# Where the weight conversions stand in ScalarE's queue: paced by key/value evictions and by gate sigmoids

## The chip, the cores and the metric

The kernel runs on one core of one Trainium2 chip. The metric is the time of one execution in microseconds (us), as the device measures it. TensorE (PE) multiplies matrices, VectorE (DVE), ScalarE (ACT) and GpSimd (POOL) do elementwise work, and SyncE (SP) issues the transfers. Each engine takes its own instructions strictly in the order of its own list. The order of these lists is made when the program is built: a scheduler sorts the instructions by priorities and by the dependences that the code declares.

## The reference

Three layers follow one another, on 4 batches of 576 positions, with 512 features (8 heads of 64):

```
x  = attention(rotate(q), rotate(k), v)            # 8 heads, softmax over 576 positions
xk = mu_k*x + (1-mu_k)*x_prev ; xr = mu_r*x + (1-mu_r)*x_prev   # x_prev: x one position earlier
x  = sigmoid(xr @ w_r) * (relu(xk @ w_k)**2 @ w_v)               # 512 -> 1024 -> 512, and the gate
u  = x + (relu(x^T @ w_tok1) @ w_tok2)^T                         # token mixing, 576 -> 256 -> 576
out = u + relu(u @ w_ch1) @ w_ch2                                # channel mixing, 512 -> 1536 -> 512
```

The weights come as 64-bit floats. The kernel turns each into a pair of a high and a low part, and every product of that kind is made of three matmuls (high x high, high x low, low x high).

## The kernel before, in words

Each batch is cut into two halves of 288 positions, which gives 8 chunks. The span has four stretches. Up to about 417 us attention runs, with the key/value products of chunks 0 to 4 in between. Then come the key/value products of chunks 5, 6 and 7 ("K/V stage", `kvr_gen`), then the gate and token mixing of the batches ("gate stage", `gate_gen` and `tok_gen`), and from about 605 us channel mixing (`ch_gen`).

For a chunk of the K/V stage, four slices `xs` of the mixed input are made, each on a chain `a`, `f`, `xs` high, `xs` low over ACT, DVE and POOL. TensorE makes 8 accumulators `kp` of 12 matmuls each. ScalarE evicts each with a Relu into `t` and squares it into the high part of `k`; POOL squares it again into `q`, and the low part of `k` is `q` minus the high part (on POOL for chunk 5, on DVE for chunks 6 and 7). TensorE then makes 4 accumulators `vp` of 24 matmuls, which ScalarE evicts into `vt`. There are four PSUM buffers for these accumulators.

For the gate, each batch half needs four slices `xs` by such a chain, in which the buffers `a` and `f` exist once, so that a new `f` waits until POOL has read the one before. Then 4 accumulators `rp` of 12 matmuls follow, each evicted by a Sigmoid into `q`. Token mixing of a batch is a chain of transposes (`trp`, evicted into `ytk`), products `t1p` (into `h`) and products `t2p` (added to `y` on DVE), in two halves.

A weight piece is converted in `Conv.stage` in four steps. It is loaded into `words` (SP). ScalarE copies it into a buffer `cv` (L215 of before); three DVE instructions put the bits together (L222, L226, L228). ScalarE writes the high part into `parts`, and DVE subtracts to get the low part (L111). Pieces of the channel weights also have their largest value taken (L233, a few tiny ones), and are scaled by it (L82 on ScalarE, L246 on DVE). `Conv.step` issues the next step of two pieces. `cv` has three buffers.

The group "conv1" is issued during the K/V stage and "conv2" during the gate stage. `SPREAD` sets how much K/V work is emitted between two steps of conv1, and the loop on `PACE` and `STEP` how much gate and token work between two steps of conv2. This is the order in which the code emits them; the scheduler may place them elsewhere. `Conv` has a means against that: where `after` names an entry of `last`, the ScalarE copy of a piece is put behind the instruction that the entry holds when the step is emitted. No engine waits more by it, it is only an order in ScalarE's list.

Of the kernel before, what the change touches and what calls it, by code (L numbers as in the profile page):

```python
# [13 lines left out]
AF = mybir.ActivationFunctionType  # L14
# [14 lines left out]

PV_AT = {7: 0, 12: 1}  # L30

HELD, LATE = 5, 2

UNIT = [(0, 256), (256, 320)]

# [1 line left out]

CW, HALF, TWICE = DCH // 2, KC // 2, 3

PACE, STEP, REST, SPREAD = (24, 28), 1, 8, 60  # L40

RAW, LOW = 3, "P"

# [28 lines left out]
def body(tc, kin, qin, vw, tabs, ident, mu, w_k, w_v, w_r, w_t1, w_t2, w_c1, w_c2, out):  # L72
# [41 lines left out]
    with ctx:  # L114
# [634 lines left out]
        def kvr_gen(seq, ready):  # L749

            xs_of = {}
            ld_of = {}

            def load(n):
                if n < len(seq) and n not in ld_of and ready(seq[n]):
                    kind, b, c = seq[n]
                    ld_of[n] = xT[b]
                    xs_of[n] = []

            def lerp(n):  # L760
                if (n < len(seq) and n in ld_of and len(xs_of[n]) < KD
                        and seq[n][1] * NP + len(xs_of[n]) in a_done):
                    xs_of[n].append(lerp_slice(ld_of[n], seq[n][2] * HS, len(xs_of[n]), 0))

            pend = []

            def tick():
                for x in pend:
                    x[0] -= 1
                while pend and pend[0][0] <= 0:  # L770
                    pend.pop(0)[1]()

            def later(*fs):
                for n, f in fs:
                    pend.append([n, f])
                pend.sort(key=lambda x: x[0])

            for n, (kind, b, c) in enumerate(seq):
                while n not in ld_of:
                    load(n)  # L780
                    tick()
                    yield 0
                if len(xs_of[n]) < KD:
                    if not xs_of[n]:
                        yield 0
                    while len(xs_of[n]) < KD:
                        lerp(n)
                        tick()
                        yield 0
                while n == HELD and not wide:  # L790
                    tick()
                    yield 0
                xs = xs_of[n]
                k2 = [None] * KF
                for m in range(KF):
                    p = accps("kp")
                    for kk in range(KD):
                        with ahead(PRI["kvpe"]):
                            mm3(p[:, 0:HS], wk[m // 4][kk], m % 4, xs[kk], kk == 0, kk == KD - 1)
                        tick()  # L800
                        yield 3

                    def ev1(p=p, m=m):
                        k2[m] = P["t"].tile([128, HS], F32, tag="t", name="t")
                        act.activation(out=k2[m], in_=p[:, 0:HS], func=AF.Relu)  # L805

                    def ev2(m=m):
                        t, k2[m] = k2[m], P["k2"].tile([128, 2, HS], F32R, tag="k2", name="k2")
                        act.activation(out=k2[m][:, 0], in_=t, func=AF.Square)
                        q = P["q"].tile([128, HS], F32, tag="q", name="q")  # L810
                        tt("P", q, t, t, ALU.mult)
                        tt("D" if second else "P", k2[m][:, 1], q, k2[m][:, 0].bitcast(F32), ALU.subtract)
                    later((1, ev1), (2, ev2))
                load(n + 1)
                half.append(n)
                for m in range(KD):
                    p = accps("vp")
                    for kf in range(KF):
                        with ahead(PRI["kvpe"]):
                            mm3(p[:, 0:HS], wv[kf // 4][kf % 4], m, k2[kf], kf == 0, kf == KF - 1)  # L820
                        if kf == 1:
                            load(n + 1)
                        if kf == 4:
                            lerp(n + 1)
                        tick()
                        yield 3

                    def ev(p=p, m=m, b=b, c=c):
                        vt = P["vt"].tile([128, HS], F32, tag="vt", name="vt")
                        copy("A", vt, p[:, 0:HS])  # L830
                        sp.dma_start(vd[b][c][:, m], vt)
                    later((1, ev))
            while pend:
                tick()
# [141 lines left out]
        def cv_t():  # L976
            return cv_p.tile([128, S], I32, tag="cv", name="cv")

        c2_a = c2_part(0, HALF)
        cv = Conv(cv_t, [wr, t1, t2], "conv1", low="D", then="out")  # L980
        def gate_gen(b):

            y = y_p[b].tile([128, KD, S], F32, tag="y", name="y")
# [3 lines left out]
            for c in range(2):  # L987
                o = c * HS
                sp.dma_start(y[:, :, o:o + HS], vd[b][c])
                yield 1  # L990
                xs = []
                for kk in range(KD):
                    a = P["a"].tile([128, HS], F32, tag="a", name="a")
                    copy("A", a, x[:, kk, o:o + HS], om_s[:, 1, kk:kk + 1])
                    f = P["f"].tile([128, HS], F32, tag="f", name="f")
                    dve.scalar_tensor_tensor(out=f, in0=x[:, kk, o + 1:o + HS + 1], scalar=mu_s[:, 1, kk:kk + 1], in1=a,
                                             op0=ALU.mult, op1=ALU.add)
                    if c == 0:
                        t = P["xs"].tile([128, 2, HS], F32R, tag="xs", name="xs")
                    else:  # L1000
                        if kk % 2 == 0:
                            two = M["uhl"].tile([128, 2, 2, HS], F32R, tag="uhl", name="xs")
                        t = two[:, kk % 2]
                    copy("A", t[:, 0], f)
                    tt("P", t[:, 1], f, t[:, 0].bitcast(F32), ALU.subtract)
                    xs.append(t)
                    yield 2
                cc = slice(c * HS, (c + 1) * HS)

                def fin(m, p):  # L1010
                    q = P["q"].tile([128, HS], F32, tag="q", name="q")
                    act.activation(out=q, in_=p[:, 0:HS], func=AF.Sigmoid)
                    tt("P", y[:, m, cc], q, y[:, m, cc], ALU.mult)

                for m in range(KD):
                    p = tps("rp")
                    for kk in range(KD):
                        mm3(p[:, 0:HS], wr[kk], m, xs[kk], kk == 0, kk == KD - 1)
                    fin(m, p)
                    yield 12  # L1020
# [33 lines left out]
        c2_b = c2_part(HALF, KC)  # L1054
        for nm, n in (("ytk", 1), ("h1", 2), ("uhl", 2), ("hs", 3), ("ht", 2), ("st", 2), ("top", 1)):
            M[nm] = top("m_" + nm, n)
        cv, cv3 = Conv(cv_t, [c1_w[0], c2_a], "conv2", low="D"), Conv(cv_t, [c1_w[1], c2_b], "conv3", low="D", after="hs")
        def all_max(m):

            p = tps("mp")  # L1060
# [144 lines left out]
        while B - 1 not in g_done or B - 2 not in u_done or not cv.done():  # L1205
# [1 line left out]
            if B - 2 not in u_done:  # L1207
                tok.advance(PACE[1])
            n += 1
            if n % STEP == 0 and not cv.done():  # L1210
                cv.step()
        n = 0
        ch = Stream(ch_gen())
# [78 lines left out]
```

## Time and profile before

| | |
|---|---|
| median of 3 runs | 917.3 us (915.67, 917.3, 920.0) |
| the profiled execution | 915.29 us, of which the span from the first to the last instruction is 913.0 us |
| TensorE busy | 846.9 us, 93% of the span |
| VectorE, ScalarE, GpSimd busy | 641.4 us, 516.6 us, 481.8 us |
| mean granted TensorE clock | 0.976 of full speed |

A matmul's record is longer than its share of the time, since matmuls overlap: back to back, 128x288 matmuls start every 0.13 us, and each record lasts 0.29 us. So the number of matmuls in a stretch tells more than TensorE's busy time.

### The profile page before, as it was taken

The page shows a single profiled execution, that of the slowest core. Times are in us where ns is not written, and L with a number is a line of the kernel's source. Part 1 is how long each engine was busy: PE and PEld are TensorE (multiplying, and loading weights), DVE is VectorE, ACT ScalarE, POOL GpSimd, SP SyncE. Part 2 cuts the span into 40 slices and gives each one's busy share as a digit, 9 for nine tenths or more (in the row PEclk, how much of TensorE's full clock was granted, in tenths as well). Part 3 has the DMA queues.
Part 4 walks back from the last instruction along what each step waited for, and adds up shares of the span by engine and source line. Part 5 has one row for each costly group of instructions (what it writes and reads, how often), then busy time and mean ns, then how long its engine had stood idle before and what let it go on. Part 6 is the DMA issues. An engine that isn't in the chain of part 4 may idle for free.

```text
span 913.0 us, 18803 instructions
## 1 busy us (share of the span) xinstructions
PE 846.9 (93%) x7004; PEld 728.9 (80%) x7004; DVE 641.4 (70%) x1468; ACT 516.6 (57%) x1155; POOL 481.8 (53%) x506
## 2 busy tenths in 40 slices
PE   8999778898887799999899899999999999999998
PEld 5788657776776678798799899988878888888876
DVE  6899789787898788847947887545798355546232
ACT  4898668776767678754546665444455322323221
POOL 5999969888788665356523554521222222222221
PEclk9999869999989999999999999999999999999999
DMA  8895389999999978889134430001230001001000
GB/s 235 271 329 166 98 193 187 196 208 168 230 195 171 203 121 157 161 173 378 46 115 152 165 126 19 1 1 36 76 93 24 1 1 53 27 27 43 11 27 27
DMA packets 168651, 112.07 MB, mean 123 GB/s; under 512 B 132720, under 2 KB 148208, under 8 KB 168048
## 3 DMA queue, kind: packets, MB, share of 16 engines
q1 hardware_dynamic: 168560, 110.87, 49.0%
q8 instruction: 55, 0.90, 0.4%
q14 instruction: 36, 0.29, 0.1%
HBM read 60.90 MB, written 14.16 MB: 82 GB/s over the span
## 4 chain that ended last, share of the span: by engine, by line
PE 56%; DVE 16%; POOL 10%; ACT 6%; issue 6%; DMA 5%; SPq 1%; DVEq 0%; ACTq 0%; POOLq 0%
PE co L737 5%; PE c1p L737 5%; PE c1p L738 5%; PE c1p L739 5%; PE co L738 5%; PE co L739 5%; POOL rq L111 3%; DVE p L511 3%; DVE nm L470 2%; PE S L452 2%; POOL rk L111 2%; DMA rq<-in_qin_dram 2%; PE vp L737 2%; PE pv L609 2%; PE kp L737 2%
## 5 line engine op out<-in xcount | busy, mean ns | idle before, releaser
L111 POOL TENSOR_TENSOR hs<-ht,hs 128x288 f16<-128x288 f32 x96 | 73.3, 764 | 229.6 <-DVE ht L1171 115.5
L1167 ACT ACTIVATE hs<-c1p,top 128x288 f16<-128x288 f32 x96 | 47.7, 497 | 161.7 <-PE c1p L739 161.7
L470 DVE TENSOR_REDUCE nm<-S 128x1 f32<-128x576 f32 x144 | 104.2, 749 | 20.5 <-PE S L452 19.8
L738 PE MATMUL c1p<-uhl,parts 128*128 128x288 f16 x384 | 109.8, 286 | 0.0
L739 PE MATMUL c1p<-uhl,parts 128*128 128x288 f16 x384 | 109.7, 286 | 0.0
L737 PE MATMUL c1p<-uhl,parts 128*128 128x288 f16 x384 | 109.5, 286 | 0.0
L738 PE MATMUL co<-hs,parts 128*128 128x288 f16 x384 | 108.7, 286 | 0.0
L739 PE MATMUL co<-hs,parts 128*128 128x288 f16 x384 | 108.6, 286 | 0.0
L737 PE MATMUL co<-hs,parts 128*128 128x288 f16 x384 | 105.1, 286 | 0.3 <-ACT hs L1167 0.3
L737 PE MATMUL kp<-xs,parts 128*128 128x288 f32 x256 | 81.9, 322 | 12.5 <-ACT t L805 6.6
L452 PE MATMUL S<-kq 64*128 64x288 f32 (+1 forms) x696 | 77.9, 325 | 14.2 <-DVE den L498 3.9
L737 PEld LDWEIGHTS <-parts 128*128 128x128 f16 x768 | 75.0, 98 | 19.3 <-issue 0.5
L738 PEld LDWEIGHTS <-parts 128*128 128x128 f16 x768 | 75.1, 98 | 18.8
L739 PEld LDWEIGHTS <-parts 128*128 128x128 f16 x768 | 75.2, 98 | 18.6
L1171 DVE TENSOR_SCALAR ht<-c1p,top 128x288 f32<-128x288 f32 x60 | 30.9, 515 | 77.7 <-ACT hs L1167 77.7
L452 PEld LDWEIGHTS S<-kq 64*128 64x128 f32 (+1 forms) x696 | 61.4, 200 | 28.9 <-issue 12.8
L737 PE MATMUL vp<-k,parts 128*128 128x288 f32 x256 | 77.6, 306 | 7.0 <-ACT vt L80 3.6
L111 POOL TENSOR_TENSOR q<-t 128x288 f32<-128x288 f32 x64 | 53.1, 833 | 57.4 <-ACT t L805 54.4
L738 PE MATMUL kp<-xs,parts 128*128 128x288 f32 x256 | 77.7, 304 | 0.0
L738 PE MATMUL vp<-k,parts 128*128 128x288 f32 x256 | 77.0, 301 | 0.1
L739 PE MATMUL kp<-xs,parts 128*128 128x288 f32 x256 | 77.1, 301 | 0.0
L511 DVE SCALAR_TENSOR_TENSOR p<-es,rc,p 128x576 f16<-128x576 f32 x60 | 67.2, 1123 | 12.2 <-ACT p L82 12.1
(158 smaller groups left out, 2484.0 us busy)
## 6 DMA issues: line engine op xcount, KB each, us to landing
rq<-in_qin_dram SPq DMA_DIRECT2D x30, 320.0 KB, 4.0
rk<-in_kin_dram SPq DMA_DIRECT2D x30, 288.0 KB, 3.7
words<-in_w_c_dram SPq DMA_DIRECT2D x16, 384.0 KB, 3.2
words<-in_w_c_dram SPq DMA_DIRECT2D x12, 512.0 KB, 3.8
vr<-in_vw_dram SPq DMA_DIRECT2D x16, 320.0 KB, 3.6
xd<-xT SPq DMA_DIRECT2D x16, 288.5 KB, 2.7
xT<-xd SPq DMA_DIRECT2D x4, 1154.0 KB, 5.6
vd<-vt SPq DMA_DIRECT2D x32, 144.0 KB, 2.3
```

Source lines behind the costliest of these rows:

```text
L111: return (pool if e == "P" else dve).tensor_tensor(o, a, b, op=op)
L452: o = pe.matmul(S_t[j][:, h, 0:HS], lhsT=a[l, 128 * m:128 * m + 128], rhs=b[l, h * HS:(h + 1) * HS], start=(n == 0), stop=(n == 2))
L470: last["max"] = dve.tensor_reduce(out=nm, in_=S_t[j][:, :, 0:HS], op=ALU.max, axis=AX.XY, negate=True)
L511: o = last["lo"] = dve.scalar_tensor_tensor(out=t[:, 1], in0=e_t.pop(j), scalar=sum_t[j], in1=t[:, 0], op0=ALU.mult, op1=ALU.subtract)
L609: pe.matmul(p[l, 0:n], lhsT=v[:, a, l], rhs=ts[x][:, c, :], start=(i == 0), stop=(i == len(prods) - 1))
L737: pe.matmul(p, lhsT=wh, rhs=t[:, 0], start=first, stop=False)
L738: pe.matmul(p, lhsT=wh, rhs=t[:, 1], start=False, stop=False)
L739: pe.matmul(p, lhsT=wl, rhs=t[:, 0], start=False, stop=last)
L1167: last["hs"] = act.activation(out=h[:, 0], in_=p[:, 0:HS], func=AF.Relu, scale=g)
L1171: dve.tensor_scalar(out=f, in0=p[:, 0:HS], scalar1=g, scalar2=0.0, op0=ALU.mult, op1=ALU.max)
```

## The change

The high part's copy of each conv1 piece is put behind the newest eviction of the K/V stage (the Square of a `k` or the copy into `vt`, kept in `last["kv"]`), that of each conv2 piece behind the newest gate Sigmoid (`last["gate"]`). Two of the six pieces of the first half of the second channel weight move from conv2 to conv1. `SPREAD` goes from 60 to 45, and conv2 steps at every second turn of its loop instead of at each.

```diff
-HELD, LATE = 5, 2
+HELD, LATE, EARLY = 5, 2, 2
...
-PACE, STEP, REST, SPREAD = (24, 28), 1, 8, 60
+PACE, STEP, REST, SPREAD = (24, 28), 1, 8, 45
...
-                        act.activation(out=k2[m][:, 0], in_=t, func=AF.Square)
+                        last["kv"] = act.activation(out=k2[m][:, 0], in_=t, func=AF.Square)
...
-                        copy("A", vt, p[:, 0:HS])
+                        last["kv"] = act.activation(out=vt, in_=p[:, 0:HS], func=AF.Copy)
...
-        c2_a = c2_part(0, HALF)
-        cv = Conv(cv_t, [wr, t1, t2], "conv1", low="D", then="out")
+        cv = Conv(cv_t, [wr, t1, t2, c2_part(0, EARLY)], "conv1", low="D", after="kv", then="out")
...
-                    act.activation(out=q, in_=p[:, 0:HS], func=AF.Sigmoid)
+                    last["gate"] = act.activation(out=q, in_=p[:, 0:HS], func=AF.Sigmoid)
...
-        cv, cv3 = Conv(cv_t, [c1_w[0], c2_a], "conv2", low="D"), Conv(cv_t, [c1_w[1], c2_b], "conv3", low="D", after="hs")
+        cv, cv3 = Conv(cv_t, [c1_w[0], c2_part(EARLY, HALF)], "conv2", low="D", after="gate"), Conv(cv_t, [c1_w[1], c2_b], "conv3", low="D", after="hs")
...
-            if n % STEP == 0 and not cv.done():
+            if n % 2 == 0 and not cv.done():
                 cv.step()
```

The lists of all engines are the same up to the end of attention, and alike again in the channel stage. Three places show what moves.

**ScalarE at the start of chunk 5.** In the list of before, the first conversions stand ahead of the evictions `t<-kp` of chunk 5 and then among them:

```order
L80 ACTIVATE vt<-vp 128x288 x2
L215 ACTIVATE cv<-words 128x512 x3
L805 ACTIVATE t<-kp 128x288 x2
L809 ACTIVATE k_6579<-t 128x288
L809 ACTIVATE k_6608<-t 128x288
L805 ACTIVATE t<-kp 128x288
L80 ACTIVATE parts<-cv 128x512
L809 ACTIVATE k_6629<-t 128x288
```

In the changed list all eight `t` and `k` of chunk 5 come first, and the first conversion stands behind the first `vt` of chunk 5, 18 rows further down:

```order
L809 ACTIVATE k_6761<-t 128x288
L80 ACTIVATE xs<-f 128x288 x3
L830 ACTIVATE vt<-vp 128x288
L215 ACTIVATE cv<-words 128x512
L830 ACTIVATE vt<-vp 128x288 x2
L215 ACTIVATE cv<-words 128x512 x2
L80 ACTIVATE parts<-cv 128x512
L805 ACTIVATE t<-kp 128x288
```

The whole of conv1 has moved behind chunk 5, among the evictions of chunks 6 and 7.

**DVE at the same place.** In the list of before, the last eviction of attention (`xT<-pv`) is followed by 21 conversion instructions before the first `f` of chunk 6 (L724); the first of them:

```order
L615 TENSOR_SCALAR xT<-pv,sc 128x320
L222 TENSOR_SCALAR cv<-cv 128x512
L226 SCALAR_TENSOR_TENSOR cv<-words,cv 128x512
L222 TENSOR_SCALAR cv<-cv 128x512 x2
L228 SCALAR_TENSOR_TENSOR cv<-words,cv 128x512
L226 SCALAR_TENSOR_TENSOR cv<-words,cv 128x512 x2
```

In the changed list `xT<-pv` is followed by three pairs of `f` and `xs` of chunk 6; the conversions begin after the fourth `f` and then alternate with the low parts of `k` of chunk 6:

```order
L724 SCALAR_TENSOR_TENSOR f<-xT,mu_s,a 128x288
L222 TENSOR_SCALAR cv<-cv 128x512
L226 SCALAR_TENSOR_TENSOR cv<-words,cv 128x512
L228 SCALAR_TENSOR_TENSOR cv<-words,cv 128x512
L222 TENSOR_SCALAR cv<-cv 128x512
L226 SCALAR_TENSOR_TENSOR cv<-words,cv 128x512
L222 TENSOR_SCALAR cv<-cv 128x512
L111 TENSOR_TENSOR parts<-cv,parts 128x512
L228 SCALAR_TENSOR_TENSOR cv<-words,cv 128x512
L226 SCALAR_TENSOR_TENSOR cv<-words,cv 128x512
L111 TENSOR_TENSOR k_6983<-q,k_6983 128x288
```

So the slices of chunk 6 no longer stand behind conversions, but the low parts of its `k`, and the slices of chunk 7, now do.

**DVE at the start of the gate stage.** In the list of before, the chain's `f` (L996) stand between conversions of conv2 from the first one on:

```order
L996 SCALAR_TENSOR_TENSOR f<-xT,mu_s,a 128x288
L222 TENSOR_SCALAR cv<-cv 128x384
L226 SCALAR_TENSOR_TENSOR cv<-words,cv 128x384 x2
L228 SCALAR_TENSOR_TENSOR cv<-words,cv 128x384 x2
L996 SCALAR_TENSOR_TENSOR f<-xT,mu_s,a 128x288
L233 TENSOR_REDUCE rows<-cv 128x1 x2
```

In the changed list (where the line is L995) the `f` of the first batch stand together, and conv2 begins after them:

```order
L111 TENSOR_TENSOR k_7530<-q,k_7530 128x288
L995 SCALAR_TENSOR_TENSOR f<-xT,mu_s,a 128x288 x9
L111 TENSOR_TENSOR ytk<-trp,ytk 128x256 x2
L995 SCALAR_TENSOR_TENSOR f<-xT,mu_s,a 128x288
L222 TENSOR_SCALAR cv<-cv 128x384 x2
L226 SCALAR_TENSOR_TENSOR cv<-words,cv 128x384
L111 TENSOR_TENSOR ytk<-trp,ytk 128x256
```

The pieces of conv2 thus begin later and reach further. Before, ScalarE's list has the copies of the first six ahead of the first of the gate's 32 Sigmoids, and the last high parts behind 16 of them. Now the first copies stand behind 8 Sigmoids and the last high parts behind 30.

## Rows read from the trace of the kernel before

**Rows 1.** The page: busy time, share of the span and instructions of each engine.

```profile
PE 846.9 (93%) x7004; PEld 728.9 (80%) x7004; DVE 641.4 (70%) x1468; ACT 516.6 (57%) x1155; POOL 481.8 (53%) x506
```

**Rows 2.** Stretches: length, busy of PE, PEld, DVE, ACT, POOL (count), PE clock, DMA.

```profile
417.25:446.33 29.08, 23.36 (x167) 22.04 (x165) 28.68 (x46) 17.91 (x44) 21.29 (x20) 0.99 0.60 223
446.33:473.40 27.07, 27.07 (x194) 27.07 (x195) 19.33 (x39) 13.30 (x32) 10.49 (x12) 0.95 0.40 121
473.40:498.70 25.30, 25.30 (x192) 25.15 (x190) 14.45 (x30) 15.44 (x36) 8.85 (x12) 1.00 0.40 128
...
498.70:604.40 105.70, 99.40 (x750) 96.17 (x750) 74.06 (x159) 57.02 (x147) 52.11 (x60) 1.00 0.22 72
...
613.00:913.00 300.00, 295.70 (x2414) 238.88 (x2412) 164.51 (x410) 104.43 (x229) 73.34 (x96) 1.00 0.10 34
```

**Rows 3.** Timeline of TensorE from 417 us: start, length, idle before and its releaser.

```profile
417.25 0.40 PE L737 MATMUL kp<-xs,parts 128*128 128x288 f32 x1
...
434.40 0.40 PE L737 MATMUL vp<-k,parts 128*128 128x288 f32 x1 [1.65 <-ACT t L805]
446.33 0.61 PE L737 MATMUL kp<-xs,parts 128*128 128x288 f32 x1 [3.55 <-ACT vt L80]
...
447.22 0.44 PE L737 MATMUL kp<-xs,parts 128*128 128x288 f32 x1
447.46 0.44 PE L738 MATMUL kp<-xs,parts 128*128 128x288 f32 x1
```

**Rows 4.** Timeline of ScalarE in the same stretch.

```profile
417.40 1.79 ACT L215 ACTIVATE cv<-words 128x512 f32<-128x512 f32 x3
419.09 0.70 ACT L805 ACTIVATE t<-kp 128x288 f32<-128x288 f32 x2
...
444.81 1.17 ACT L215 ACTIVATE cv<-words 128x576 f32<-128x576 f32 x2
445.89 0.69 ACT L80 ACTIVATE vt<-vp 128x288 f32<-128x288 f32 x2
```

**Rows 5.** Timelines of DVE and POOL; POOL's groups from 418 to 440 us.

```profile
418.17 0.43 DVE L222 TENSOR_SCALAR cv<-cv 128x512 int32<-128x512 int32 x1 [0.25 <-ACT cv L215]
418.63 0.69 DVE L226 SCALAR_TENSOR_TENSOR cv<-words,cv 128x512 int32<-128x512 int32 x1
...
434.58 0.41 DVE L228 SCALAR_TENSOR_TENSOR cv<-words,cv 128x256 int32<-128x256 int32 x1
...
441.10 0.28 DVE L222 TENSOR_SCALAR cv<-cv 128x256 int32<-128x256 int32 x1
...
476.18 0.46 DVE L111 TENSOR_TENSOR k<-q,k 128x288 fp32r<-128x288 f32 x1 [8.38 <-POOL q L111]
...
475.48 0.67 POOL L111 TENSOR_TENSOR q<-t 128x288 f32<-128x288 f32 x1 [10.25 <-ACT t L805]
...
L111 POOL TENSOR_TENSOR k<-q,k 128x288 fp32r<-128x288 f32 x8 | 9.0, 1139 | 0.0
L111 POOL TENSOR_TENSOR q<-t 128x288 f32<-128x288 f32 x8 | 7.7, 971 | 9.2 <-ACT t L805 9.2
```

**Rows 6.** Stretches of ten us in the gate stage, columns as in group 2.

```profile
510.00:520.00 10.00, 6.91 (x46) 5.71 (x45) 8.75 (x20) 6.08 (x17) 5.30 (x7) 1.00 0.57 212
520.00:530.00 10.00, 10.00 (x80) 10.00 (x79) 8.94 (x19) 5.08 (x14) 3.71 (x4) 1.00 0.33 105
530.00:540.00 10.00, 8.57 (x64) 7.91 (x63) 9.94 (x20) 5.88 (x16) 6.10 (x6) 1.00 0.14 35
...
550.00:560.00 10.00, 9.25 (x67) 8.49 (x67) 8.90 (x22) 4.48 (x13) 1.88 (x4) 1.00 0.15 41
...
590.00:600.00 10.00, 10.00 (x82) 10.00 (x81) 3.48 (x9) 2.21 (x8) 1.61 (x2) 1.00 0.00 0
```

**Rows 7.** ScalarE's wait for the gate chain; the chain's `f` on DVE as a group.

```profile
512.95 0.44 ACT L80 ACTIVATE xs<-f 128x288 fp32r<-128x288 f32 x1 [3.53 <-DVE f L996]
...
L996 DVE SCALAR_TENSOR_TENSOR f<-xT,mu_s,a x31: 502/519/1075, 486.7 to 584.4; 128x288 f32<-128x288 f32 x31
```

## The prediction, made before the changed kernel was run

> **What bounds the kernel now.** I read the page's busy times first: TensorE is busy for 93% of the span, no other engine for more than 70% [rows 1]. So time can only come from the places where TensorE has nothing to do or runs slowly, and the next view to read is the one by stretches. In the channel stage, from 613 us, TensorE is busy for 295.7 of 300 us [rows 2]; the lists there are alike before and after, so those 300 us stay. Up to 417 us the lists are the same. What can change lies between 417.25 and 604.4 us.
>
> The chunk 7 stretch gives TensorE's pace: 192 matmuls in 25.30 us, 0.1318 us each [rows 2]. Measured by it, the first K/V stretch (417.25 to 446.33 us) is poor: 167 matmuls are worth 22.0 us and took 29.08, so 7.1 us are lost. The second (446.33 to 473.40 us) has 194, worth 25.6 us, in 27.07: 1.5 us lost, at a granted clock of 0.95 [rows 2]. The timeline of TensorE shows both. It waits 1.65 us at 434.40 and 3.55 us at 446.33, and after that second wait the matmuls start 0.24 us apart (447.22, 447.46) [rows 3], which is the pace of the lower level, 1.2 GHz, against 0.13 us at 2.4 GHz; before it the engine had had little to do for ten us.
>
> Why was there nothing to do? DVE is busy for 28.68 of those 29.08 us, with 46 instructions, of which 38 belong to conversions [rows 2]. The slices `xs` of chunk 6 stand behind 21 of these in DVE's list. ScalarE puts conversions first too: three copies of 1.79 us delay the first evictions of chunk 5 to 419.09, and the evictions that TensorE awaits at 446.33 start at 445.89, behind a pair of conversions of 1.17 us [rows 4]. GpSimd suffers as well: its `q` takes 0.97 us on the mean and its `k` 1.14 us while DVE is busy, against 0.67 us for a `q` beside an idle DVE [rows 5].
>
> In the gate stage a stretch without gaps has about 80 matmuls in 10 us; 510 to 520 has 46, 530 to 540 has 64 and 550 to 560 has 67 [rows 6]. That is 34, 16 and 13 missing, at 0.125 us each 4.25, 2.0 and 1.6 us. DVE is busy for 8.75 to 9.94 of the 10 us there. The wait behind the first gap is named on ScalarE: `xs` at 512.95 waited 3.53 us for the chain's `f` [rows 7], which stood behind conversions of conv2.
>
> **The change, part by part.**
>
> *Conversions behind the evictions of chunk 5.* DVE's list then has only lerp work of chunk 6 after 417 us. POOL makes eight `q` and eight `k`; at the crowded means that is 7.7 + 9.0 = 16.7 us [rows 5], and a `q` beside idle DVE takes 0.67, so it will be below that. Even so POOL, starting by 419, is through with them and the few lerp steps between by about 438, while TensorE has work until 417.25 + 22.0 = 439.25. The first three slices of chunk 6 are ready early; the last two `a` follow POOL's last `k` and need some 3 us for their chain, about 439 to 441 at the crowded price and 435 at the other, against 440.4, when the fourth slice is first needed. I take no loss here: minus 7.1 us, and minus 1.5 us since the clock has no cause to fall. Bounds: nothing gained if chunk 6's slices were late for another reason, which no row shows; 8.6 us if all goes.
>
> *The same conversions among chunks 6 and 7.* This is the debt that the move incurs. DVE's changed list has, from the first conversion to the last slice of chunk 7, 53 instructions: 38 of conversions, 8 low parts `k`, 4 `xs`, 3 `f`. At uncrowded prices [rows 5] the conversions are 12 two-input ones of 512 wide at 0.69, 15 of 256 wide at 0.41, 4 and 5 shifts at 0.43 and 0.28, and one of each kind of 576 wide, at 576/512 of these prices 0.48 and 0.78: 18.8 us; the 15 others at 0.46 (`k`, `xs`) and 0.52 (`f`, [rows 7]) make 7.1. Together 25.9 us. The crowded bound is the old stretch itself: 28.7 us for the 38 and six lerp steps, plus nine more at 0.6, 34.1 us. The time there is: from the first `vt` of chunk 5 at about 437 us to the fourth slice of chunk 7, due 192 matmuls and nine more after 439.25, at 465.7: 28.7 us. So the debt is between nothing and 5.4 us. POOL was busy for 21.3 of 29.1 us when DVE was slow, 73%; beside chunk 6 it has eight `q` and two `a`, some 6.5 of 28.7 us, 23%. By that share the price is 25.9 + 8.2 x 23/73 = 28.5 us, just inside. I take 1.0 us for hand-overs between ScalarE and DVE. The old second stretch supports this end: DVE was busy for 19.3 of 27.1 us there, conversions included, and TensorE lost nothing but clock.
>
> The Trainium skill, page "SBUF — State Buffer", section "Who interferes with whom", speaks against it: a DVE instruction with two SBUF inputs and a GpSimd instruction that reads SBUF exclude each other, and the second waits for the whole of the first. By that rule each of the eight `q` could cost DVE its whole 0.67 us, 25.9 + 5.4 = 31.3 us, a debt of 2.6 us instead of 1.0. The slower prices of group 5 agree with the rule in kind; how often the two meet, they don't tell.
>
> Sum of the K/V stage: -7.1 - 1.5 + 1.0 = -7.6 us (bounds -8.6 and -3.2).
>
> *conv2 behind the Sigmoids, at half the pace.* The eight `xs` of the first batch are now made without conversions between, so the first gap goes: -4.25 us. The two later gaps (3.6 us) came from DVE's load, and that load does not fall, it spreads. Three pairs that were converted ahead of the first Sigmoid now come after it, and two pieces of the second weight leave; eight pieces of 384 and four of 512 remain, against two and six before. A piece of 512 is five DVE instructions, 0.43 + 4 x 0.69 = 3.2 us [rows 5], one of 384 about 2.4, so 32.0 us instead of 24.0: 74 [rows 2] + 8 = 82 us in about 100, 82% throughout, where the gaps arose at 87% and more and where 520 to 530, at 89%, had none [rows 6]. I put the loss over these 75 us at 4.9 us, between nothing and 3.6 x 75/40 = 6.8. Sum of the gate stage: -4.25 - 3.6 + 4.9 = -3.0 us (bounds -7.9 and about -1).
>
> *Two pieces in the first group, SPREAD, the loop.* The two pieces' work is counted above (DVE has some 7 us for them during chunk 7, where it was busy for 14.5 of 25.3 us [rows 2]). SPREAD and the loop's step have no cost of their own. No engine gets a wait that it did not have; the order in ScalarE's list only decides what stands in front. What stands in front of the evictions now is at most one copy or one high part (0.6 to 0.7 us, [rows 4] has three in 1.79), and four accumulators give TensorE more than that.
>
> Total: -7.6 - 3.0 = -10.6 us on the profiled 915.3: 904.7 us. The profiled execution lies 2.0 us below the median of the three runs, so beside 917.3 this reads **906.7 us**. A measurement of this kernel tells about 0.5%, 4.6 us, from no change.
>
> **The rivals.**
>
> *The gate chain sets the pace, not the conversions.* From the second to the last, 31 `f` of the chain stand from 486.7 to 584.4 us [rows 7], 3.26 us per link, though one `f` is 0.52 us. If each link keeps that price, the gate stage gains nothing and only the K/V part arrives: -7.6, so 909.7 us. For it: TensorE waits for `xs` there. Against it: with few conversions, 590 to 600 us, TensorE has 82 matmuls [rows 6].
>
> *The debt is paid in full.* DVE works at the crowded prices beside chunk 6 as well: -8.6 + 5.4 = -3.2 us, and with it nothing from the gate stage: 914.1 us. For it: DVE is the engine that the moved work loads. Against it: POOL's small share there.
>
> *Everything goes.* All of 8.6 and 7.9 us: -16.5, 900.8 us.
>
> *The last pieces hold up token mixing (slower).* The last high parts now stand behind 30 of 32 Sigmoids. Each half of token mixing hands over to DVE three times (`ytk`, `h`, `y`), and at the end few gate products are left to fill in. Before, DVE is busy for 3.5 us in 590 to 600 [rows 6]; now two pairs of 512 wide are due there. conv2's pieces reach over the last four halves, twelve handovers. If each waited for a pair's step, 2 x 0.69 us [rows 5], that is 16.6 us, and -10.6 becomes +6.0: 923.3 us. The sign turns at 10.6 us, 0.88 us for each handover; where gate products fill the gaps, as before, it is a fraction of that.
>
> **How the numbers follow.** The forecast (-9 to -14 us) gets 0.48, the chain 0.20, everything 0.09, the debt 0.14, the tail 0.09. From 901.5 to 915 us the range takes in the forecast, the chain and the debt, and leaves out the other two, 0.18. Faster by over 0.5% (below 912.7): the first three, 0.77, less a little for spill, 0.76. Within 0.5%: the debt and what spills, 0.16. Slower: 0.08.
>
> **What the changed profile would show.** Right: chunk 6's `kp` start at about 439 instead of 446.3 us with no spacing of 0.24 us behind them; chunk 7's start near 466 instead of 473.4; the stretch of the first two rounds of gate products has no window of 46 matmuls; POOL's `k` of chunk 5 take nearer to 0.8 than 1.14 us; the channel stage stays 300 us to within one. Wrong: TensorE waiting for `xs` or for an eviction around 455 to 470 us (debt), `f` still 3.3 us apart (chain), or gaps just ahead of the channel stage behind `ytk`, `h` and the last conversions (tail).

## The result, and the profile after

The changed kernel took 904.0 us (median of four executions, 903.3 to 908.2) beside 918.2 us for the kernel before (four, 915.7 to 920.0): ratio 0.986, 95% interval 0.982 to 0.990. Timed again with more executions (last group of experiments) it took 908.8 beside 916.0 us, ratio 0.994, interval 0.991 to 0.997. The change is faster both times, within the predicted range; the two sizes, 14 and 7 us, are further apart than their intervals allow, and the stage times below say which part of that is the change. The profiled execution took 908.2 us with a span of 906.0 us.

The page's busy row, and then the stretches of the K/V stage and of the channel stage (length, busy time of PE, PEld, DVE, ACT and POOL with counts, TensorE clock, DMA share, GB/s), answer to [rows 1] and [rows 2]:

```profile
PE 843.6 (93%) x7004; PEld 726.6 (80%) x7004; DVE 636.2 (70%) x1468; ACT 513.9 (57%) x1155; POOL 476.2 (53%) x506
```

```profile
417.00:441.00 24.00, 24.00 (x182) 23.69 (x182) 7.04 (x11) 9.56 (x23) 14.82 (x21) 1.00 0.92 342
441.00:466.70 25.70, 25.54 (x193) 25.31 (x192) 24.18 (x51) 18.68 (x46) 10.35 (x10) 1.00 0.20 60
466.70:492.00 25.30, 24.54 (x185) 24.29 (x184) 17.87 (x33) 14.88 (x35) 11.86 (x12) 1.00 0.36 124
...
606.00:906.00 300.00, 295.66 (x2413) 238.83 (x2411) 164.59 (x410) 104.36 (x229) 73.33 (x96) 1.00 0.10 34
```

TensorE is now busy for the whole of the first stretch, where DVE's 28.7 us have shrunk to 7.0. DVE's conversions stand in the second, 24.2 of 25.7 us, and TensorE does not mind. The clock is 1.00 in all three. The channel stage has not moved. TensorE's timeline (start, length, idle time before it and its releaser) at the first matmuls of chunks 6 and 7, and the one wait inside chunk 7, answer to [rows 3]; below them POOL's groups from 419 to 441 us, which answer to [rows 5]:

```profile
440.85 0.30 PE L737 MATMUL kp<-xs,parts 128*128 128x288 f32 x1
440.98 0.29 PE L738 MATMUL kp<-xs,parts 128*128 128x288 f32 x1
...
466.70 0.29 PE L737 MATMUL kp<-xs,parts 128*128 128x288 f32 x1
...
482.43 0.40 PE L738 MATMUL vp<-k,parts 128*128 128x288 f32 x1 [0.76 <-DVE k L111]
```

```profile
L111 POOL TENSOR_TENSOR k<-q,k 128x288 fp32r<-128x288 f32 x8 | 6.6, 832 | 0.0
L111 POOL TENSOR_TENSOR q<-t 128x288 f32<-128x288 f32 x8 | 5.4, 696 | 8.1 <-ACT t L805 8.1
```

No row at chunk 6's start names a wait now, and matmuls start 0.13 us apart instead of 0.24.

Absolute times can't be laid beside each other: the attention stage, whose lists are the same, ended at 417.4 us in the profile of before and at 419.0 us here. Each stage is therefore counted from its own first event. Four rows carry this: the last eviction of attention (`xT<-pv`, DVE), the last `vt` of the K/V stage, the first Sigmoid (`q<-rp`) and the first operand of the channel stage (`hs<-c1p`), all three on ScalarE. First those of the kernel before, then those of the changed kernel, then those of a second profile of the changed kernel:

```profile
417.36 0.55 DVE L615 TENSOR_SCALAR xT<-pv,sc 128x320 f32<-128x320 f32 x1 [14.38 <-PE pv L609]
498.82 0.41 ACT L80 ACTIVATE vt<-vp 128x288 f32<-128x288 f32 x1 [0.19 <-PE vp L739]
502.53 0.41 ACT L1012 ACTIVATE q<-rp 128x288 f32<-128x288 f32 x1
612.93 0.50 ACT L1167 ACTIVATE hs<-c1p,top 128x288 f16<-128x288 f32 x1 [2.37 <-PE c1p L739]
```

```profile
419.00 0.55 DVE L615 TENSOR_SCALAR xT<-pv,sc 128x320 f32<-128x320 f32 x1 [14.38 <-PE pv L609]
493.44 0.41 ACT L830 ACTIVATE vt<-vp 128x288 f32<-128x288 f32 x1 [2.65 <-PE vp L739]
497.16 0.41 ACT L1011 ACTIVATE q<-rp 128x288 f32<-128x288 f32 x1
605.89 0.50 ACT L1166 ACTIVATE hs<-c1p,top 128x288 f16<-128x288 f32 x1 [2.35 <-PE c1p L739]
```

```profile
422.67 0.55 DVE L615 TENSOR_SCALAR xT<-pv,sc 128x320 f32<-128x320 f32 x1 [14.38 <-PE pv L609]
497.06 0.41 ACT L830 ACTIVATE vt<-vp 128x288 f32<-128x288 f32 x1 [2.58 <-PE vp L739]
500.78 0.41 ACT L1011 ACTIVATE q<-rp 128x288 f32<-128x288 f32 x1
609.52 0.50 ACT L1166 ACTIVATE hs<-c1p,top 128x288 f16<-128x288 f32 x1 [2.37 <-PE c1p L739]
```

In the two profiles of the changed kernel attention ended 3.67 us apart, but from there to the last `vt` it is 74.44 and 74.39 us, and from the first Sigmoid to the first `hs` 108.73 and 108.74 us. Counted like this a stage of the changed kernel repeats to 0.1 us between two profiles, where whole executions of this kernel scatter over ten.

| us | to chunk 6's first `kp` | to chunk 7's | to the last `vt` | gate stage | attention's end to first `hs` |
|---|---|---|---|---|---|
| before | 28.97 | 55.84 | 81.5 | 110.4 | 195.6 |
| changed | 21.85 | 47.70 | 74.4 | 108.7 | 186.9 |
| difference | -7.1 | -8.1 | -7.0 | -1.7 | -8.7 |

(The first three columns count from attention's end, the fourth from the first Sigmoid.) So the change is worth 8.7 us, 7.0 of them in the K/V stage. On 916 us that is a ratio of 0.9905, between the two measurements.

Ten-us windows of the changed gate stage, which answer to [rows 6]:

```profile
510.00:520.00 10.00, 10.00 (x80) 9.76 (x78) 9.08 (x21) 6.25 (x20) 6.07 (x8) 1.00 0.26 79
520.00:530.00 10.00, 9.08 (x67) 8.15 (x66) 9.49 (x19) 5.58 (x16) 4.36 (x5) 1.00 0.22 75
530.00:540.00 10.00, 9.43 (x73) 9.19 (x72) 8.94 (x20) 7.04 (x18) 6.87 (x8) 1.00 0.35 125
540.00:550.00 10.00, 9.63 (x75) 9.03 (x73) 9.94 (x24) 5.82 (x17) 5.10 (x7) 1.00 0.29 93
550.00:560.00 10.00, 9.70 (x76) 9.63 (x76) 9.97 (x22) 6.94 (x19) 5.08 (x6) 1.00 0.15 54
560.00:570.00 10.00, 9.42 (x73) 9.18 (x72) 8.82 (x23) 5.77 (x14) 4.66 (x5) 1.00 0.18 52
570.00:580.00 10.00, 9.27 (x74) 9.06 (x74) 9.06 (x21) 6.49 (x17) 5.50 (x7) 1.00 0.30 94
580.00:590.00 10.00, 9.39 (x74) 9.18 (x73) 9.46 (x24) 4.06 (x13) 2.46 (x3) 1.00 0.30 79
590.00:600.00 10.00, 9.80 (x79) 9.56 (x77) 5.12 (x16) 3.00 (x10) 1.60 (x2) 1.00 0.01 2
```

The hole of 46 matmuls is gone. In its place nearly every window lacks four to seven of 80 and one lacks 13, as long as DVE is 88 to 100% busy: 49 in all, at 0.125 us 6.1 us.

### The profile page after: what moved, and what is told of

It is laid out like the page before. It is cut to its first block, busy times and chain, and to the rows that moved or that the text cites. A ratio compares the mean times of both kernels' runs of the same rounds, so it can differ in the third digit from the quotient of the medians.

```text
span 906.0 us, 18800 instructions
## 1 busy us (share of the span) xinstructions
PE 843.6 (93%) x7004; PEld 726.6 (80%) x7004; DVE 636.2 (70%) x1468; ACT 513.9 (57%) x1155; POOL 476.2 (53%) x506
## 4 chain that ended last, share of the span: by engine, by line
PE 48%; DVE 16%; POOL 6%; ACT 6%; issue 5%; DMA 4%; SPq 1%; DVEq 0%; ACTq 0%; POOLq 0%
PE co L737 5%; PE c1p L737 5%; PE c1p L738 5%; PE c1p L739 5%; PE co L738 5%; PE co L739 5%; DVE p L511 4%; PE pv L609 2%; DVE nm L470 2%; PE vp L737 2%; PE vp L738 2%; PE vp L739 2%; DMA pt<-p 2%; PE kp L737 1%; PE S L452 1%
## 5 line engine op out<-in xcount | busy, mean ns | idle before, releaser
L738 PE MATMUL co<-hs,parts 128*128 128x288 f16 x384 | 108.7, 286 | 0.0
L737 PE MATMUL kp<-xs,parts 128*128 128x288 f32 x256 | 80.1, 316 | 9.0 <-ACT t L805 8.0
L1170 DVE TENSOR_SCALAR ht<-c1p,top 128x288 f32<-128x288 f32 x60 | 30.9, 516 | 77.6 <-ACT hs L1166 76.5
L737 PE MATMUL vp<-k,parts 128*128 128x288 f32 x256 | 76.5, 304 | 4.9 <-ACT vt L830 3.9
L738 PE MATMUL vp<-k,parts 128*128 128x288 f32 x256 | 76.2, 300 | 0.9 <-DVE k L111 0.9
L738 PE MATMUL kp<-xs,parts 128*128 128x288 f32 x256 | 76.3, 298 | 0.0
L739 PE MATMUL kp<-xs,parts 128*128 128x288 f32 x256 | 75.7, 296 | 0.0
```

The source lines that it names most:

```text
L737: pe.matmul(p, lhsT=wh, rhs=t[:, 0], start=first, stop=False)
L738: pe.matmul(p, lhsT=wh, rhs=t[:, 1], start=False, stop=False)
L739: pe.matmul(p, lhsT=wl, rhs=t[:, 0], start=False, stop=last)
L1170: dve.tensor_scalar(out=f, in0=p[:, 0:HS], scalar1=g, scalar2=0.0, op0=ALU.mult, op1=ALU.max)
```

## The experiments

The theory going in was the prediction's: two terms that add, K/V about -7 and gate about -3, with the two moved pieces, SPREAD and the loop of no cost of their own. The rivals: one part alone carries the gain; or the parts need one another.

**One order at a time.** Three kernels, on one chip beside a fourth told further down: the K/V order alone, the gate order alone with half pace, and the changed kernel without the K/V order. The first is before plus

```diff
-                        act.activation(out=k2[m][:, 0], in_=t, func=AF.Square)
+                        last["kv"] = act.activation(out=k2[m][:, 0], in_=t, func=AF.Square)
...
-                        copy("A", vt, p[:, 0:HS])
+                        last["kv"] = act.activation(out=vt, in_=p[:, 0:HS], func=AF.Copy)
...
-        cv = Conv(cv_t, [wr, t1, t2], "conv1", low="D", then="out")
+        cv = Conv(cv_t, [wr, t1, t2], "conv1", low="D", after="kv", then="out")
```

> The kernel before with one part of the change: conv1's copies behind the newest key/value eviction; conv2, SPREAD and the six pieces as before. Theory A (the gain is the K/V stage's): about 7 us less than before, ratio 0.992, chunk 6's first kp about 22 us after the last attention eviction instead of 29, and no half-pace matmuls behind it; the gate stage keeps a window with some 50 matmuls in 10 us. Theory B (the gain comes from the gate stage, the K/V stall would only move): within 2 us of before.

Measured: 914.4 us beside 915.1, ratio 1.0005 (0.998 to 1.003). The K/V stage is 7.3 us shorter, as the theory has it, and the gate stage 5.9 us longer, 116.3 us. Its windows from the first Sigmoid on show where:

```profile
503.30:513.30 10.00, 6.79 (x39) 5.52 (x38) 7.98 (x13) 7.61 (x21) 6.58 (x7) 0.90 0.40 147
...
553.30:563.30 10.00, 8.04 (x49) 8.03 (x50) 7.87 (x17) 5.91 (x14) 3.74 (x4) 0.83 0.08 14
```

Two holes, each with a granted clock below 1.00. The conversions pushed back in the K/V stage push conv2 back: nine pieces start their bit work on DVE after the first Sigmoid, seven before.

The gate order alone is before plus

```diff
-                    act.activation(out=q, in_=p[:, 0:HS], func=AF.Sigmoid)
+                    last["gate"] = act.activation(out=q, in_=p[:, 0:HS], func=AF.Sigmoid)
...
-        cv, cv3 = Conv(cv_t, [c1_w[0], c2_a], "conv2", low="D"), Conv(cv_t, [c1_w[1], c2_b], "conv3", low="D", after="hs")
+        cv, cv3 = Conv(cv_t, [c1_w[0], c2_a], "conv2", low="D", after="gate"), Conv(cv_t, [c1_w[1], c2_b], "conv3", low="D", after="hs")
...
-            if n % STEP == 0 and not cv.done():
+            if n % 2 == 0 and not cv.done():
```

> The kernel before with the other part: conv2's copies behind the newest gate Sigmoid, a step at every second turn; conv1 as before. Theory A: 1.5 to 4 us less than before (ratio 0.996 to 0.998), and the stall of 7 us ahead of chunk 6 stays. Theory B: 7 us or more less.

Measured: 920.4 us, ratio 1.008 (1.005 to 1.011): slower. The K/V stage is as before, and the gate stage 116.5 us. Up to 600 us it runs like the changed kernel's; then comes this window:

```profile
600.40:610.40 10.00, 4.35 (x23) 3.72 (x21) 9.13 (x27) 2.88 (x6) 0.00 (x0) 0.70 0.28 79
```

The third is the changed kernel without its K/V order:

```diff
-        cv = Conv(cv_t, [wr, t1, t2, c2_part(0, EARLY)], "conv1", low="D", after="kv", then="out")
+        cv = Conv(cv_t, [wr, t1, t2, c2_part(0, EARLY)], "conv1", low="D", then="out")
```

> The changed kernel without the order behind key/value evictions in conv1; the gate's order, the two pieces and SPREAD stay. Theory A: 7 us more than the changed kernel (about 911), chunk 6's kp 29 us after the last attention eviction. Theory B: within 2 us of the changed kernel.

Measured: 913.1 us, ratio 0.999 (0.996 to 1.002). The gate stage is the changed kernel's (108.8 us), the last `vt` comes 82.0 us after attention's end, as before. So the K/V order carries the K/V stage's 7 us (shown twice, put in and taken out), and the parts do not simply add: either order alone gains nothing.

**Both orders, without moving the two pieces.** The changed kernel with all six pieces in conv2 (and SPREAD at 60):

```diff
-HELD, LATE, EARLY = 5, 2, 2
+HELD, LATE = 5, 2
...
-PACE, STEP, REST, SPREAD = (24, 28), 1, 8, 45
+PACE, STEP, REST, SPREAD = (24, 28), 1, 8, 60
...
-        cv = Conv(cv_t, [wr, t1, t2, c2_part(0, EARLY)], "conv1", low="D", after="kv", then="out")
+        c2_a = c2_part(0, HALF)
+        cv = Conv(cv_t, [wr, t1, t2], "conv1", low="D", after="kv", then="out")
...
-        cv, cv3 = Conv(cv_t, [c1_w[0], c2_part(EARLY, HALF)], "conv2", low="D", after="gate"), Conv(cv_t, [c1_w[1], c2_b], "conv3", low="D", after="hs")
+        cv, cv3 = Conv(cv_t, [c1_w[0], c2_a], "conv2", low="D", after="gate"), Conv(cv_t, [c1_w[1], c2_b], "conv3", low="D", after="hs")
```

> Both orders as in the changed kernel, but all six pieces of the second channel weight stay in conv2 (14 pieces at half pace) and SPREAD stays 60. Theory 'the two pieces cost and bring nothing of their own' (the prediction's): the same time as the changed kernel, about 906 us, ratio to before 0.986, channel stage starting some 187 us after the last attention eviction. Theory 'conv2 at half pace has to end before token mixing does, and only the two moved pieces let it': K/V stage 7 us shorter as in the changed kernel, but at the end of the gate stage the same gaps as with the gate order alone (two windows of 10 us with about 23 matmuls in place of 75), some 7 us, so channel stage starting 194 to 195 us after the last eviction, about 914 us, ratio 0.997 to 1.000.

Measured: 914.1 us beside 915.2, ratio 0.999 (0.996 to 1.003), as the second theory had it. The K/V stage is 8.0 us shorter than before, the gate stage 116.25 us. Windows of the end, TensorE's wait there, and the low parts of conv2 as a group (first and last start):

```profile
585.47:595.47 10.00, 10.00 (x81) 10.00 (x81) 5.47 (x14) 5.04 (x12) 2.47 (x4) 1.00 0.08 28
595.47:605.47 10.00, 3.70 (x20) 3.04 (x18) 9.02 (x29) 2.95 (x7) 0.00 (x0) 0.78 0.31 79
```

```profile
600.89 0.61 PE L1061 MATMUL mp<-idn,top 128*128 128x128 f32 x2 [4.86 <-DVE top L1070]
```

```profile
L246 DVE SCALAR_TENSOR_TENSOR parts<-cv,rows,parts x14: 606/744/1168, 519.0 to 602.6; 128x384 f16<-128x384 f32 x8, 128x512 f16<-128x512 f32 x6
```

The mechanism is in the wait. The scale of the channel stage needs the largest entry of all six pieces; DVE reduces it into `top`, and the matmul `mp` that spreads it over the partitions stands in TensorE's list ahead of the last transposes of token mixing. When the last piece comes late, TensorE stands at `mp` for 4.9 us with work queued behind it, and the clock drops (0.78 on the mean of that window). The gate order alone has the same wait at `mp`, 4.9 us. In the changed kernel the last low part starts at 590.9 us, 15.0 us ahead of the first `hs`; here 8.3 us.

**The gate stage's other two parts.** The changed kernel without the order behind the Sigmoids, and with a step at each turn of the loop:

```diff
-        cv, cv3 = Conv(cv_t, [c1_w[0], c2_part(EARLY, HALF)], "conv2", low="D", after="gate"), Conv(cv_t, [c1_w[1], c2_b], "conv3", low="D", after="hs")
+        cv, cv3 = Conv(cv_t, [c1_w[0], c2_part(EARLY, HALF)], "conv2", low="D"), Conv(cv_t, [c1_w[1], c2_b], "conv3", low="D", after="hs")
```

> The changed kernel without the wait of conv2 behind the Sigmoids in ScalarE's list (half pace, the two pieces in the first group and the K/V order stay). Theory 'the gate order removes the first gap, 4.25 us': a window of about 46 matmuls in 10 us comes back just behind the first Sigmoid, gate stage 3 to 5 us longer, about 909 us, ratio 0.990. Theory 'the half pace and the smaller number of pieces do it, not the order': gate stage within 1 us of the changed kernel, about 906 us, ratio 0.986.

```diff
-            if n % 2 == 0 and not cv.done():
+            if n % 1 == 0 and not cv.done():
```

> The changed kernel with a conversion step of conv2 at each round of the loop again, not each second (the gate order and the two moved pieces stay). Theory 'the load has to be spread' (the prediction's 82% throughout): DVE is again over 95% busy in the first 40 us of gate products, gaps of 10 to 16 matmuls a window in two or three windows, gate stage 3 to 5 us longer, about 909 to 911 us, ratio 0.991 to 0.995. Theory 'pace does not matter once ScalarE has the Sigmoids first': within 1 us of the changed kernel, ratio 0.986.

Measured: 911.6 us, ratio 0.995 (0.992 to 0.998), gate stage 112.45 us; and 912.3 us, ratio 0.997 (0.994 to 1.000), gate stage 114.1 us. Without the order two holes of 49 and 48 matmuls come back, and the K/V stage is 2.1 us longer than the changed kernel's (76.5 us): twelve conv2 instructions that the order holds back now stand in DVE's list in chunk 7, and TensorE waits there for `k` four times, 1.7 us in all. The order is thus worth 5.8 us, 3.7 of them in the gate stage. With the order but at full pace there is one hole, in the second window after the first Sigmoid:

```profile
507.55:517.55 10.00, 6.77 (x34) 5.24 (x35) 9.76 (x22) 7.07 (x20) 6.15 (x7) 0.83 0.41 124
```

Here the releaser of the longest wait (1.78 us at 515.07) is DVE's `ytk`, not a conversion on ScalarE. So the order on ScalarE does not by itself remove the hole: the DVE work behind each ScalarE copy must be thinned too.

**More pieces early.** The changed kernel with all six, and with four (`EARLY` 4, run on two chips):

```diff
-HELD, LATE, EARLY = 5, 2, 2
+HELD, LATE, EARLY = 5, 2, 6
...
-        cv, cv3 = Conv(cv_t, [c1_w[0], c2_part(EARLY, HALF)], "conv2", low="D", after="gate"), Conv(cv_t, [c1_w[1], c2_b], "conv3", low="D", after="hs")
+        cv, cv3 = Conv(cv_t, [c1_w[0]], "conv2", low="D", after="gate"), Conv(cv_t, [c1_w[1], c2_b], "conv3", low="D", after="hs")
```

> The changed kernel with all six pieces of the second channel weight in the first group (conv1 has 23 pieces more DVE work than in the changed kernel by four pieces of 512, 13 us; conv2 has the eight pieces of 384 alone). By the prediction's debt (28.7 us of time, 28.5 us of work before chunk 7's slices; the pieces come after those and so fall into chunk 7 and the first gate rounds): K/V stage within 1 us of the changed kernel, gate stage 0 to 2 us shorter, 904 to 906 us, ratio 0.984 to 0.987. Rival 'the first group runs over into the gate stage': DVE busy for over 9.5 of 10 us at the first Sigmoids, first gate windows under 60 matmuls, 908 to 911 us, ratio 0.990 to 0.994.

> The changed kernel with four instead of two pieces of the second channel weight in conv1. Between 480 and 510 us of the changed kernel DVE is busy for about a third of the time. Theory A (DVE's load in the gate stage costs TensorE its gaps): the gate stage gets 1 to 2 us shorter, about 902.5. Rival (the debt is not yet paid at chunk 7): chunk 7's key/value products are held up by as much or more, 904 to 907.

> The changed kernel with four of six pieces in the first group, beside the changed kernel on the same chip. By the stage times of its first profile (K/V stage +0.6 us, gate stage -0.9 us) it is the same as the changed kernel to within 0.5 us, ratio 0.990; if the two further pieces take DVE's load off the gate stage, as the prediction's spread load has it (6.4 us of DVE in 100), 1 to 2 us faster, 0.988.

Measured: all six, 910.2 us, ratio 0.997 (0.994 to 1.000): K/V stage 2.3 us longer than the changed kernel's, gate stage 109.9, with 59 matmuls in 549.6 to 559.6 us. The rival held in place of the debt's arithmetic: the first group runs over into the gate stage. Four: 906.7 us beside 915.1, then 907.7 beside 916.0 (ratios 0.993 and 0.992); K/V +0.6, gate -0.9 and -0.9. The changed kernel on the second chip: 908.8. No difference that can be measured.

**SPREAD alone, the load alone, and the changed kernel again**, on the chip of that last run.

```diff
-PACE, STEP, REST, SPREAD = (24, 28), 1, 8, 45
+PACE, STEP, REST, SPREAD = (24, 28), 1, 8, 60
```

> The changed kernel with SPREAD at 60 as before, not 45. Prediction's theory (SPREAD has no cost of its own): stage times within 0.5 us of the changed kernel's, ratio equal to it within 0.3%. Rival: with 60 the conversions of the first group come later in ScalarE's list against K/V work, two pieces more run over into the gate stage, first Sigmoid as in the changed kernel, first gate window behind it with 60 or fewer matmuls in 10 us, gate stage 2 to 4 us longer, ratio 0.992 to 0.995.

Measured: 908.9 us, ratio 0.993 (0.990 to 0.996). The gate stage is the same to 0.1 us, but the K/V stage is 1.1 us shorter (too little to show in whole executions, 908.9 beside 908.8), and its stretches for chunks 6 and 7 have all their 194 matmuls:

```profile
444.40:469.90 25.50, 25.50 (x194) 25.45 (x193) 21.57 (x44) 17.20 (x43) 9.65 (x10) 1.00 0.24 78
469.90:495.60 25.70, 25.62 (x194) 25.39 (x192) 22.15 (x40) 16.25 (x38) 9.98 (x12) 1.00 0.33 100
```

The wait for `k` in chunk 7 is gone with it. That is all of the debt, and it came from SPREAD 45.

The load: the bit operations of conv1 and conv2 on 16 columns. The kernel leaves out the bits of the other columns.

```diff
                     m = self.room()[:, :w] if self.room else v
+                    whole = v
+                    if self.name in ("conv1", "conv2"):
+                        m, v, hw, lw = m[:, 0:16], v[:, 0:16], hw[:, 0:16], lw[:, 0:16]
...
-                        yield lambda: dve.tensor_reduce(out=rows[:, 0, o:o + 1], in_=v.bitcast(F32),
+                        yield lambda: dve.tensor_reduce(out=rows[:, 0, o:o + 1], in_=whole.bitcast(F32),
```

> The changed kernel in which the three bit operations of each conversion step of conv1 and conv2 on DVE (shift, mask and join) work on 16 columns, not 512, 384 or 256: the bits of the other columns are left out, so the values are not those of the weights; every instruction, wait and order stays. DVE loses some 18 of 32 us of conversion work in the gate stage and about half of 18.8 us in the K/V stage. Theory of the prediction (the gate stage pays for DVE's spread load, 4.9 us; the K/V stage pays a debt of 1.0 us): gate stage (first Sigmoid to first operand of the channel stage) 4 to 6 us shorter than 108.7, K/V stage 0.5 to 1 us shorter, about 6 us off in all, ratio 0.983 to 0.985. Rival (the order of hand-overs between ScalarE, DVE and GpSimd costs these gaps, not the load): both stages within 1 us of the changed kernel.

Measured: 907.4 us, ratio 0.992 (0.989 to 0.995). It tells less than it was meant to: the scheduler reordered the shorter instructions, so that the sentence "every instruction, wait and order stays" was wrong, and at the end a matmul of the channel stage came to stand ahead of the last token mixing and waited 3.4 us there (its first `hs` has 760 matmuls behind the first Sigmoid, not 785). Only the stretch ahead of that can be used. In the first 80 us from the first Sigmoid it ran 598 matmuls, the changed kernel 575: 23 more, 2.9 us. The gate chain's `f` are 2.88 us apart instead of 3.13. The K/V stage is 1.5 us shorter.

> The changed kernel, unaltered, timed again beside the kernel before and with more runs (the first comparison had four of each). If the changes of stage times in the profiles (-7.0 us K/V, -1.7 us gate) are the whole of it, the ratio is 0.9905 with -8.7 us; the first comparison's 0.9861 would be -12.8 us and would ask for something outside these stages.

Measured: 908.8 us, ratio 0.994 (0.991 to 0.997). The stage times repeat; what the first comparison has beyond 8.7 us, and the second short of it, should then lie outside the stages that the change touches. Of most of these executions there is no profile, so this is argued and not shown.

The gate stage of all of them, from the first Sigmoid to the first `hs`:

| gate stage, us | K/V order | gate order | half pace | pieces moved |
|---|---|---|---|---|
| 110.4 (before) | no | no | no | none |
| 116.3 | yes | no | no | none |
| 116.5 | no | yes | yes | none |
| 116.25 | yes | yes | yes | none |
| 112.45 | yes | no | yes | two |
| 114.1 | yes | yes | no | two |
| 108.8 | no | yes | yes | two |
| 108.7 (changed) | yes | yes | yes | two |
| 107.8 | yes | yes | yes | four |
| 109.9 | yes | yes | yes | six |

## Why the prediction was right, and where it was not

*K/V stage, -7.6 forecast, -7.0 measured.* "Minus 7.1": chunk 6's first `kp` moved by 7.12 us against attention's end. "Minus 1.5" for the clock: chunk 7's start moved by a further 1.0. The signs named for it all came: no wait at chunk 6, no 0.24 us spacing, `k` on POOL at 0.83 us instead of 1.14. One reading behind the clock's term was wrong, that the engine "had had little to do for ten us": TensorE was busy for 6.3 of the ten us ahead of 446.33. It stood still for the last 3.55 us, and the clock was at the lower level (0.50) when it began again. Without that wait it stayed at 1.00.

*The debt, 1.0 forecast, 1.1 measured, but not where it was put: the agreement is luck.* It was expected ahead of chunk 7, out of DVE's 53 instructions at 28.5 us. Their records add up to 29.5 us, above that and above the 28.7 us that there were. But DVE was busy for 25.8 us from 439.3 to 466.8 us, and chunk 7 started on time. The forecast's sum took each record for time of its own, where DVE's records overlap as TensorE's do. Here three of 0.68 us start 0.60 and 0.61 us apart:

```profile
448.05 0.68 DVE L228 SCALAR_TENSOR_TENSOR cv<-words,cv 128x512 int32<-128x512 int32 x1
448.65 0.68 DVE L111 TENSOR_TENSOR parts<-cv,parts 128x512 fp32r<-128x512 f32 x1
449.26 0.68 DVE L226 SCALAR_TENSOR_TENSOR cv<-words,cv 128x512 int32<-128x512 int32 x1
```

What was lost was lost inside chunk 7 (x185 in the third stretch above), on `k`, and it goes with SPREAD back at 60. "SPREAD and the loop's step have no cost of their own" was wrong by 1.1 us for the one and, with the sign the other way, 5.4 us for the other (114.1 against 108.7).

By the Trainium skill, "SBUF — State Buffer", "Who interferes with whom", a DVE instruction with two SBUF inputs and a GpSimd instruction that reads SBUF exclude each other; eight full waits of that kind were reckoned at a debt of 2.6 us. Where they meet, the trace agrees in kind: two bit operations of 512 columns beside POOL's `q` take 1.16 and 1.15 us; alone they take 0.69, as the low part ahead of them still does ([rows 5] has the same). First DVE's timeline, then POOL's:

```profile
443.75 0.69 DVE L111 TENSOR_TENSOR parts<-cv,parts 128x512 fp32r<-128x512 f32 x1
444.35 1.16 DVE L228 SCALAR_TENSOR_TENSOR cv<-words,cv 128x512 int32<-128x512 int32 x1
445.43 1.15 DVE L226 SCALAR_TENSOR_TENSOR cv<-words,cv 128x512 int32<-128x512 int32 x1
```

```profile
443.77 2.26 POOL L111 TENSOR_TENSOR q<-t 128x288 f32<-128x288 f32 x2 [7.37 <-ACT t L805]
```

Each of chunk 6's eight `q` met one DVE instruction, at some 0.46 us a time and not 0.67: 3.7 us more on DVE, not 5.4. DVE had room for them only because its records overlap, and the debt by the rule did not arise.

*Gate stage, -3.0 forecast, -1.7 measured: the term that was mis-sized is the spread load.* The first gap went, and so did the two later ones, 7.85 us by [rows 6]. For the spread load, "between nothing and 6.8", the forecast took 4.9; the windows above lack 6.1 us, and 6.1 - 7.85 comes close to the -1.7 that was measured. (Only roughly: these windows don't begin with the stage, and 7.85 counts three of before's.) The load itself was put too low, at 8 us more for DVE. From the first Sigmoid to the first `hs`, before and changed, it grew by 11.5:

```profile
502.53:612.93 110.40, 103.07 (x785) 99.07 (x783) 76.50 (x172) 58.29 (x153) 51.27 (x59) 1.00 0.19 63
```

```profile
497.16:605.89 108.73, 102.78 (x785) 98.86 (x783) 88.02 (x199) 60.71 (x161) 50.95 (x59) 1.00 0.24 76
```

With most of the bit work left out 2.9 of the 6.1 us came back, so about half is DVE's load, as far as that reordered kernel can tell. The rest was not taken apart.

*"The two pieces' work is counted above", "SPREAD and the loop's step have no cost of their own", and "the first gap goes" by the order.* This is the step that failed in kind, though the sum hid it. The gate term was written as one gain of the order; the runs show that it needs three parts together. The order without the half pace leaves a hole (114.1 us), the half pace without the order two (112.45), and both without the moved pieces end too late for `mp` (116.25). The two pieces are worth 7.5 us at the end of the gate stage, and the order holds 2.1 us in the K/V stage besides (without it 76.5 us there, not 74.4).

*The rivals.* The tail rival had the right place, the last pieces of conv2, and its price, 7.5 us where it acts, lies below the 10.6 us at which the sign turns; it was put on hand-overs of token mixing, and it is one wait of 4.9 us for the row maxima, with the lower clock behind it. It did not occur since the two pieces had been moved, which the forecast had not seen as the reason. The chain rival's sign, `f` 3.3 us apart, came nearly (3.13), and the total of -8.7 us lies nearer to its -7.6 than to -10.6. As a fixed price per link it fell: with less work on DVE the same chain runs at 2.88 us per link. The debt in full did not come.

*The total.* -10.6 forecast, -8.7 in the stages. The median of the first comparison, 904.0 us, lies under the forecast 906.7, the second, 908.8, above.

## What to carry to other kernels

A conversion that is taken out of the way of one stage arrives in the next, so a pacing change is to be costed up to the point where the last converted piece is used, here a reduction over all pieces whose matmul stands ahead of other work. Look for the first instruction that needs all pieces, not only for the first that needs one. Price an engine's work by the distance between starts and not by the length of its records: here 53 records of 29.5 us in all took DVE 25.8 us. And count stages from their own first event: two profiles of one kernel agreed to 0.1 us this way while their spans differed by 3.6 us.

## What was not expected of the hardware

The same list for attention ended between 414.5 and 422.8 us in fourteen profiles. Part of it is the granted clock at the start. The first 40 us, in the profile that ended attention at 416.1 us and then in one at 422.5 us:

```profile
0.00:20.00 20.00, 17.05 (x98) 9.89 (x99) 11.38 (x28) 8.31 (x17) 11.59 (x18) 1.00 0.87 244
20.00:40.00 20.00, 17.99 (x182) 15.25 (x179) 16.29 (x43) 15.68 (x33) 19.88 (x21) 1.00 0.88 290
```

```profile
0.00:20.00 20.00, 17.20 (x62) 9.71 (x63) 10.01 (x24) 6.48 (x13) 11.90 (x18) 0.77 0.88 234
20.00:40.00 20.00, 19.27 (x157) 16.08 (x158) 13.93 (x34) 14.36 (x30) 14.04 (x17) 0.89 0.66 202
```

The one has the upper level (1.00, 2.4 GHz) throughout, the other spent part of both stretches at the lower one, 1.2 GHz, and was 61 matmuls behind by 40 us. Why it falls in one execution and not in another, with the same instructions, no run here shows. The 8.3 us between these ends are as much as the change is worth, so a gain of 8.7 us can measure as 7 or as 14 when few executions are compared. That this is what happened here is not shown.
